# Rebalancing the Fourier and gate stages of a fused GFNet and gMLP block: one DMA queue in written order, copies moved between VectorE and ScalarE, the last Fourier step moved into the main loop

## The chip, the cores and the metric

The kernel runs on one core of a Trainium2 chip. The metric is the device time in microseconds, the median of several runs. A profiled execution gives the span from the first to the last instruction, which is a little shorter than the device time. The engines of the core work side by side, each through its own list of instructions in order: TensorE (PE in the profile; PEld is its weight load), VectorE (DVE), ScalarE (ACT), GpSimd (POOL) and SyncE (SP). In this kernel SP does nothing but start transfers. The kernel is written with a tile scheduler: it takes the program, works out which instruction must wait for which, and may reorder the instructions of each engine.

## The reference, cut to what matters

`x` is 2048 x 576, bf16. One branch filters the normalised `x` in the frequency domain, the other is a gated MLP whose gate mixes the 2048 rows. Their product is added to `x`.

```python
def _A_ref(x, w_r, w_i):                      # spectral filter
    X = rfft2(x) * (w_r + 1j * w_i)           # over rows (2048) and columns (576)
    return irfft2(X, s=(2048, 576))

def _B_ref(x, w_in, w_sp, b_sp, w_out):       # Fh = 2304
    z = gelu(x @ w_in)
    z1, z2 = z[..., :Fh], layernorm(z[..., Fh:])
    g = w_sp @ z2 + b_sp[:, None]             # w_sp is 2048 x 2048
    return (z1 * g) @ w_out

xn = layernorm(x)
return x + _A_ref(xn) * silu(_B_ref(xn))
```

## The kernel before

Everything works on 16 row tiles `m` of 128 rows. The stages, by the names in the code:

- `ln1`, `p0`: normalise `x`, transpose it into `xnT`, multiply by the column DFT (`CDSD`), store to `Ad` in HBM.
- `p1`, `p23`, `p4`, `p5`: the 2048-point DFT over rows in two factors, the product with `w_r`, `w_i`, and the way back. Between the steps the data goes through HBM (`Ad`, `Bd`, `Ed`, `Yd`), which reshuffles it.
- `z2`: the gate half, `gelu(xn @ w_in)` and its layernorm, kept in `Z2`.
- `z1`, `main`: for each of 4 blocks `q` of 512 rows and 18 column tiles `fi`: the value half, then `w_sp @ z2`, bias, product into `U`. `outm`: the last matmul, silu, product with the filtered `x`, sum, store.

The parts that the change touches:

```python
sizes = dict(A0=12288, ..., AIN=4*8*L, TT=8*L, BES=2*8*L, ZT=5*512)   # one SBUF arena AR
SLAB = [reg("AIN", 0, 8192)..., reg("A0", 0, 8192)...]                # w_sp, transposed, two blocks
TMP  = [reg("ZT", (3 + i) * 512, 512) for i in range(2)]
...
XC = [load_x(0)]                              # four loads of one row tile, SP queue
nc.sync.dma_start(out=CDSD, ...)
for c in range(1, 4): XC.append(load_x(c))    # four row tiles in one load each
for g in range(2):                            # gate weights, ACT queue
    nc.scalar.dma_start(out=WIN2[:, 0:KS-1, sl], ...)
    nc.scalar.dma_start(out=WIN2[0:KT, KS-1, sl], ...)
nc.scalar.dma_start(out=G1, ...); nc.scalar.dma_start(out=MM, ...)
nc.scalar.dma_start(out=G4, ...); nc.scalar.dma_start(out=CESO, ...)

def ln1(ms):
    ...                                       # bn_stats, bn_aggr on VectorE
    rs = rstd_of(mv, n, f"l1_{n}")            # (var + eps) ** -0.5 on GpSimd
    ...                                       # nm = -mean * rs, two GpSimd instructions
    for i, m in enumerate(ms):
        nc.scalar.activation(out=xn[:, 0:D], in_=XC[...], func=ACT.Identity, bias=nm, scale=rs)
        for ks in range(KS): nc.tensor.transpose(pt[:, ks, :], xn[:, ks*P:(ks+1)*P], ident[:])
        nc.vector.tensor_copy(out=xnT[:, m, :, :], in_=pt[:])

def p0(m):    # 10 matmuls, ScalarE copy into one of 3 STG buffers, SP store to Ad
def p1(ch):   # SP load from Ad; 8 matmuls; copies half ScalarE, half VectorE; SP store to Bd
def p23(ch):  # SP load from Bd; per 2 slices: 2 matmuls, 2 VectorE products with the
              # spectral weights, 4 matmuls, ScalarE copy; SP stores to Ed
def p4(ch):   # SP load from Ed; 3 x 8 matmuls, each group copied into V by VectorE
def p5(j):    # 6 matmuls, ScalarE copy, VectorE sum and difference, 2 SP stores to Yd
def z2(m):
    for n in range(NZC):                      # 6 pieces of 384 columns
        ...                                   # 5 matmuls into ph
        nc.scalar.activation(out=Z2[m][...], in_=ph[:], func=ACT.Gelu_apprx_tanh)
        nc.vector.bn_stats(out=st[:, n, :], in_=Z2[m][...])
    nc.vector.bn_aggr(...); rs = rstd_of(mv, 1, "l2")
    nc.vector.tensor_scalar(out=Z2[m][:], in0=Z2[m][:], scalar1=mean, scalar2=rs, ...)

for ms in ([0], [1], [2, 3], [4, 5, 6, 7], [8, 9, 10, 11], [12, 13, 14, 15]):
    ln1(ms)
    for m in ms: p0(m)
load_w(0); load_w(1)
for ch in range(4): p1(ch)
for ch in range(4): p23(ch)
for ch in range(4): p4(ch)
for m in range(MT): z2(m)
for j in range(MT): p5(j)
load_slab(0); ...; load_slab(1)
nc.sync.dma_start(out=WOUT, ...)
z1(0)
for k in range(NK):                           # NK = 72
    if k + 1 < NK: z1(k + 1)                  # 5 matmuls of 512 columns
    main(k)                                   # 16 matmuls of 512 columns, 2 VectorE instructions
    if fi == 0 and q > 0:
        for i in range(4): outm(q - 1, i)     # 36 matmuls of 288 columns each
        ...
```

The scheduler mixes `z2` into `p1`, `p23` and `p4`, so TensorE has work while a Fourier step waits for its transfer.

Of the kernel before, what the change touches and what calls it, by code (L numbers as in the profile page):

```python
# [80 lines left out]
def kernel(  # L81
# [56 lines left out]
    make_identity(nc, ident[:])  # L138
    mhalf = pers.tile([P, MT], F32)
# [3 lines left out]
                 AIN=4 * 8 * L, TT=8 * L, BES=2 * 8 * L, ZT=5 * 512)  # L143
# [14 lines left out]
    SLAB = [reg("AIN", 0, 8192).rearrange("p (m t) -> p m t", m=MT),  # L158
# [12 lines left out]
    TMP = [reg("ZT", (3 + i) * 512, 512) for i in range(2)]  # L171
# [10 lines left out]
    def load_x(c):  # L182
        t = AIN[c][:, 0:4 * D].rearrange("p (m d) -> p m d", m=4)
        if c == 0:
            for i in range(4):
                nc.sync.dma_start(out=t[:, i, :], in_=xv[:, i, :])
        else:
            nc.sync.dma_start(out=t, in_=xv[:, 4 * c:4 * c + 4, :])
        return t

    XC = [load_x(0)]
# [4 lines left out]
    wv = B_w_in[0:(KS - 1) * P, :].rearrange("(k p) f -> p k f", p=P)  # L196
    for g in range(2):
        sl = slice(g * Fh // 2, (g + 1) * Fh // 2)
        gl = slice(Fh + g * Fh // 2, Fh + (g + 1) * Fh // 2)
        nc.scalar.dma_start(out=WIN2[:, 0:KS - 1, sl], in_=wv[:, :, gl])  # L200
        nc.scalar.dma_start(out=WIN2[0:KT, KS - 1, sl], in_=B_w_in[(KS - 1) * P:D, gl])
    nc.scalar.dma_start(out=G1, in_=cd_g1.ap().rearrange("p (s k) -> p s k", s=N2))
    nc.scalar.dma_start(out=MM, in_=cd_mm.ap().rearrange("p (a k) -> p a k", a=3))
    nc.scalar.dma_start(out=G4, in_=cd_g4.ap().rearrange("p (s k) -> p s k", s=N2))
    nc.scalar.dma_start(out=CESO, in_=cd_ceso.ap().rearrange("p (a c l) -> p a c l", a=NLC, c=2))
# [8 lines left out]
    def ln1(ms):  # L214
        n = len(ms)
        mv = small.tile([P, n, 2], F32, tag=f"mv{n}", bufs=3)
        for i, m in enumerate(ms):
            st = small.tile([P, 2, 6], F32, tag="st1", bufs=4)
            for h in range(2):
                nc.vector.bn_stats(out=st[:, h, :], in_=XC[m // 4][:, m % 4, h * H2:(h + 1) * H2])  # L220
            nc.vector.bn_aggr(out=mv[:, i, :], in_=st[:])
        rs = rstd_of(mv, n, f"l1_{n}")
        nm = small.tile([P, n], F32, tag=f"nm{n}", bufs=3)
        nc.gpsimd.tensor_tensor(out=nm[:], in0=mv[:, :, 0], in1=rs[:], op=ALU.mult)
        nc.gpsimd.tensor_scalar(out=nm[:], in0=nm[:], scalar1=-1.0, scalar2=0.0, op0=ALU.mult, op1=ALU.add)
        for i, m in enumerate(ms):
            xn = XN[m % 3]
            nc.scalar.activation(out=xn[:, 0:D], in_=XC[m // 4][:, m % 4, :], func=ACT.Identity,  # L228
                                 bias=nm[:, i:i + 1], scale=rs[:, i:i + 1])
            pt = psh.tile([P, KS, P], BF16, tag="h")  # L230
            for ks in range(KS):
                nc.tensor.transpose(pt[:, ks, :], xn[:, ks * P:(ks + 1) * P], ident[:])  # L232
            nc.vector.tensor_copy(out=xnT[:, m, :, :], in_=pt[:])  # L233
# [15 lines left out]

    def p1(ch):  # L250
        ain = AIN[ch]
        nc.sync.dma_start(out=ain, in_=rowv(Ad)[:, ch * 8 * L:(ch + 1) * 8 * L])
        av = ain.rearrange("p (s l) -> p s l", s=8)
        bs = BES[ch % 2]
        bv = bs.rearrange("p (s l) -> p s l", s=8)
        for i in range(0, 8, 2):
            pa = psa.tile([P, 2, 512], F32, tag="a")
            for j in range(2):
                nc.tensor.matmul(pa[:, j, 0:L], lhsT=G1[:, ch * 8 + i + j, :], rhs=av[:, i + j, :], start=True, stop=True)
            if i % 4 == 0:  # L260
                nc.scalar.activation(out=bv[:, i:i + 2, :], in_=pa[:, :, 0:L], func=ACT.Identity)
            else:
                nc.vector.tensor_copy(out=bv[:, i:i + 2, :], in_=pa[:, :, 0:L])
        nc.sync.dma_start(out=rowv(Bd)[:, ch * 8 * L:(ch + 1) * 8 * L], in_=bs)
# [7 lines left out]

    def p23(ch):
        ain = AIN[ch].rearrange("p (h l) -> p h l", h=8)
        nc.sync.dma_start(out=ain, in_=colv(Bd)[:, ch * 8:(ch + 1) * 8, :])
        for i in range(0, 8, 2):
            hh = ch * 8 + i
            if hh % 4 == 0 and hh >= 8:
                load_w(hh // 4)
            wt = WCH[(hh // 4) % 2]  # L280
            tt = TT[(i // 2) % 2]
            pa = psa.tile([P, 2, 512], F32, tag="a")
            for j in range(2):
                nc.tensor.matmul(pa[:, j, 0:L], lhsT=MM[:, 0, :], rhs=ain[:, i + j, :], start=True, stop=True)
            for c in range(2):
                nc.vector.tensor_tensor(out=tt[:, c, :, :], in0=pa[:, :, 0:L], in1=wt[:, c, hh % 4:hh % 4 + 2, :], op=ALU.mult)  # L286
            pb = psa.tile([P, 2, 512], F32, tag="a")
            for j in range(2):
                for c in range(2):
                    nc.tensor.matmul(pb[:, j, 0:L], lhsT=MM[:, 1 + c, :], rhs=tt[:, c, j, :], start=(c == 0), stop=(c == 1))  # L290
            es = BES[ch % 2].rearrange("p (h l) -> p h l", h=8)
            nc.scalar.activation(out=es[:, i:i + 2, :], in_=pb[:, :, 0:L], func=ACT.Identity)
            if i % 4 == 2:
                nc.sync.dma_start(out=colv(Ed)[:, hh - 2:hh + 2, :], in_=es[:, i - 2:i + 2, :])

    def p4(ch):
        ain = AIN[ch]
        nc.sync.dma_start(out=ain, in_=rowv(Ed)[:, ch * 8 * L:(ch + 1) * 8 * L])
        av = ain.rearrange("p (s l) -> p s l", s=8)
        for lc in range(NLC):  # L300
            pa = psa.tile([P, 2, 4, P], F32, tag="a")
            for i in range(8):
                nc.tensor.matmul(pa[:, i // 4, i % 4, :], lhsT=av[:, i, LC0[lc]:LC0[lc] + P], rhs=G4[:, ch * 8 + i, :],
                                 start=True, stop=True)
            nc.vector.tensor_copy(out=V[:, lc, :, ch * 8:ch * 8 + 8, :].rearrange("p c s t -> p s c t"),  # L305
                                  in_=pa[:].rearrange("p a s (c t) -> p (a s) c t", c=2))
# [16 lines left out]

    def z2(m):
        st = small.tile([P, NZC, 6], F32, tag="st2")
        mv = small.tile([P, 1, 2], F32, tag="mvz")
        for n in range(NZC):
# [4 lines left out]
            nc.scalar.activation(out=Z2[m][:, n * ZC:(n + 1) * ZC], in_=ph[:], func=ACT.Gelu_apprx_tanh)  # L332
            nc.vector.bn_stats(out=st[:, n, :], in_=Z2[m][:, n * ZC:(n + 1) * ZC])  # L333
        nc.vector.bn_aggr(out=mv[:, 0, :], in_=st[:])
# [4 lines left out]
    for ms in ([0], [1], [2, 3], [4, 5, 6, 7], [8, 9, 10, 11], [12, 13, 14, 15]):  # L339
        ln1(ms)  # L340
        for m in ms:
            p0(m)
    load_w(0)
    load_w(1)
    for ch in range(4):
        p1(ch)
    for ch in range(4):
        p23(ch)
    for ch in range(4):
        p4(ch)  # L350
    for m in range(MT):
        z2(m)
    for j in range(MT):
        p5(j)

    wspv = B_w_sp.rearrange("t (b p) -> t b p", p=P)

    def load_slab(q):
        for i in range(4):
            t0 = q * 512 + i * P  # L360
            nc.sync.dma_start_transpose(out=SLAB[q % 2][:, :, i * P:(i + 1) * P], in_=wspv[t0:t0 + P, :, :])

    load_slab(0)
    nc.sync.dma_start(out=BB, in_=B_b_sp.rearrange("(a s) -> a s", a=1).to_broadcast((P, S)))
    for i in range(2):
        nc.gpsimd.memset(WIN1[i][KT:P, KS - 1, :], 0.0)
    load_slab(1)
    nc.sync.dma_start(out=WOUT, in_=B_w_out.rearrange("(f p) d -> p f d", p=P))

    steps = [(q, fi) for q in range(NQ) for fi in range(FT)]  # L370

    def z1(k):
# [3 lines left out]
        if fi % WG == 0:  # L376
            fs = slice(fi * P, (fi + WG) * P)
            nc.sync.dma_start(out=wb[:, 0:KS - 1, :], in_=wv[:, :, fs])
            nc.sync.dma_start(out=wb[0:KT, KS - 1, :], in_=B_w_in[(KS - 1) * P:D, fs])
# [34 lines left out]
    z1(0)  # L414
    NK = len(steps)
    for k in range(NK):
        q, fi = steps[k]
        if k + 1 < NK:
            z1(k + 1)
        main(k)  # L420
        if fi == 0 and q > 0:
            if q + 1 < NQ:
                pass
            for i in range(4):
                outm(q - 1, i)
            if q + 1 < NQ:
                load_slab(q + 1)
    for i in range(4):
        outm(NQ - 1, i)
# [30 lines left out]
```

## Time and profile before

| | before |
|---|---|
| device time, median of 6 runs | 598.63 us (598.07 to 601.3) |
| span of the profiled execution | 596.9 us |
| TensorE busy | 546.5 us, 92% |
| VectorE busy | 243.7 us, 41% |
| ScalarE busy | 145.8 us, 24% |
| GpSimd busy | 23.8 us, 4% |
| moved by the transfers | 59.46 MB |

A share of busy time is an average over the stages. The page also has a view of the span in 40 slices, in which VectorE stands at 9 tenths for several slices of the first third, and at 2 or 3 tenths in the last two thirds. A matmul's duration in the profile is its latency; neighbours overlap, so rates are taken from runs of many matmuls in the chain of work. A wait is given with the engine and line that waited, what it waited for, the sum in us, how often, and the longest.

### The profile page before, as it was taken

To read this page: it belongs to the slowest core of one execution; us is meant where nothing else is said; L and a number is where in the kernel's file an instruction comes from. 1 tells how busy PE (TensorE), PEld (TensorE's weight loads), DVE (VectorE), ACT (ScalarE), POOL (GpSimd) and SP (SyncE) were. 2 spreads that over 40 slices of the span, in tenths; PEclk is the share of its full clock that TensorE was granted. 3 is DMA by queue.
4 is the path that set the end of the run, shared out by engine and by line. 5 is a ranking of instruction groups with operands and counts; after the bars stand their busy time and mean duration, and the time that the engine had idled before them with its cause. 6 is when DMAs were issued, how large, how long until landed. Compare 5 with 4: busy or idle time off the path is not lost.

```text
span 596.9 us, 7781 instructions
## 1 busy us (share of the span) xinstructions
PE 546.5 (92%) x3128; PEld 299.5 (50%) x3128; DVE 243.7 (41%) x468; ACT 145.8 (24%) x258; POOL 23.8 (4%) x69
## 2 busy tenths in 40 slices
PE   0299899997979959999999999999999999999996
PEld 0177455555645424444744444674444475444465
DVE  3522789997976202222322222232222223222223
ACT  0386556662533101111111111111111101111101
POOL 4200100010010000000000000000000000000000
PEclk9999999998989969999999999999999999999999
DMA  9923686654715871113731111751111114111002
GB/s 312 329 82 95 235 239 170 162 160 163 140 30 116 199 226 31 30 31 78 155 87 30 40 50 31 129 136 56 31 30 31 30 33 118 30 31 30 1 9 71
DMA packets 80964, 59.46 MB, mean 100 GB/s; under 512 B 36768, under 2 KB 75552, under 8 KB 80672
## 3 DMA queue, kind: packets, MB, share of 16 engines
q1 hardware_dynamic: 79136, 53.68, 33.6%
q10 hardware_dynamic: 1792, 5.29, 2.6%
q8 instruction: 24, 0.39, 0.3%
q14 instruction: 12, 0.10, 0.1%
HBM read 38.74 MB, written 11.82 MB: 85 GB/s over the span
## 4 chain that ended last, share of the span: by engine, by line
PE 78%; DMA 8%; DVE 8%; ACT 2%; issue 1%; POOL 1%; SPq 1%; ACTq 0%; DVEq 0%; POOLq 0%
PE pg L390 41%; PE ph L382 13%; PE po L404 12%; PE ph L330 5%; PE pa L241 3%; DVE st L333 3%; DMA AR<-in_A_x_dram 2%; DVE AR L305 2%; DMA AR<-in_B_w_out_dram 2%; DVE AR L286 1%; PE pa L314 1%; PE pb L290 1%; DMA Ed<-AR 1%; DVE z L336 1%; DMA AR<-in_A_w_i_dram 1%
## 5 line engine op out<-in xcount | busy, mean ns | idle before, releaser
L390 PE MATMUL pg<-AR,z 128*128 128x512 bf16 x1152 | 262.8, 380 | 0.0
L390 PEld LDWEIGHTS <-z 128*128 128x128 bf16 x1152 | 113.1, 98 | 135.3 <-issue 1.9
L393 DVE TENSOR_TENSOR AR<-pg,AR 128x512 bf16<-128x512 f32 x72 | 49.8, 691 | 236.9 <-PE pg L390 236.9
L384 ACT ACTIVATE AR<-ph 128x512 bf16<-128x512 f32 x72 | 43.0, 597 | 272.2 <-PE ph L382 272.2
L382 PE MATMUL ph<-xnT,AR 128*128 128x512 bf16 x360 | 91.2, 384 | 0.0
L330 PE MATMUL ph<-RW,xnT 128*128 128x384 bf16 x480 | 88.2, 328 | 0.0
L404 PE MATMUL po<-AR,RW 128*128 128x288 bf16 x576 | 72.4, 288 | 6.7 <-DMA AR<-in_B_w_out_dram 6.7
L404 PEld LDWEIGHTS <-RW 128*128 128x128 bf16 x576 | 56.7, 98 | 22.5 <-issue 7.0
L330 PEld LDWEIGHTS <-xnT 128*128 128x128 bf16 x480 | 46.8, 98 | 26.4 <-issue 0.9
L332 ACT ACTIVATE z<-ph 128x384 bf16<-128x384 f32 x96 | 46.9, 491 | 41.7 <-PE ph L330 41.5
L382 PEld LDWEIGHTS <-AR 128*128 128x128 bf16 x360 | 35.6, 99 | 41.9 <-issue 0.8
L333 DVE BATCH_NORM_STATS2 st<-z 128x6 f32<-128x384 bf16 x96 | 48.1, 542 | 8.2 <-ACT z L332 7.9
L394 DVE TENSOR_TENSOR RW<-AR 128x512 bf16<-128x512 bf16 x72 | 30.6, 425 | 7.4 <-DVE AR L393 0.5
L409 DVE SCALAR_TENSOR_TENSOR AR<-TH,po 128x576 bf16<-128x576 f32 x16 | 12.1, 755 | 46.4 <-ACT TH L408 46.4
L232 PE MATMUL pt<-ident,AR 128*128 128x128 bf16 x80 | 6.3, 230 | 26.4 <-ACT AR L228 26.3
L408 ACT ACTIVATE TH<-po 128x576 f32<-128x576 f32 x16 | 10.4, 651 | 76.5 <-PE po L404 76.5
L241 PE MATMUL pa<-AR,xnT 128*128 128x289 bf16 x160 | 22.6, 298 | 0.3 <-ACT AR L244 0.2
L286 DVE TENSOR_TENSOR AR<-pa,AR 128x578 bf16<-128x578 f32 x32 | 22.6, 746 | 0.1
L232 PEld LDWEIGHTS <-AR 128*128 128x128 bf16 x80 | 5.1, 102 | 27.5 <-ACT AR L228 27.3
L241 PEld LDWEIGHTS <-xnT 128*128 128x128 bf16 x160 | 15.7, 101 | 5.8 <-DVE xnT L233 0.6
L314 PE MATMUL pa<-AR 128*128 128x289 bf16 x96 | 14.9, 298 | 3.8 <-DVE AR L320 3.5
L220 DVE BATCH_NORM_STATS2 st<-AR 128x6 f32<-128x288 bf16 x32 | 12.6, 428 | 12.8 <-DMA AR<-in_A_x_dram 12.8
(40 smaller groups left out, 212.0 us busy)
## 6 DMA issues: line engine op xcount, KB each, us to landing
AR<-in_B_w_in_dram SPq DMA_DIRECT2D x24, 384.0 KB, 3.5
AR<-in_A_x_dram SPq DMA_DIRECT2D x20, 144.0 KB, 2.7
AR<-in_B_w_out_dram SPq DMA_DIRECT2D x1, 2592.0 KB, 10.5
AR<-in_A_w_r_dram SPq DMA_DIRECT2D x16, 144.5 KB, 3.5
AR<-in_A_w_i_dram SPq DMA_DIRECT2D x16, 144.5 KB, 3.9
Ad<-AR SPq DMA_DIRECT2D x16, 144.5 KB, 2.7
AR<-Ad SPq DMA_DIRECT2D x4, 578.0 KB, 5.6
Bd<-AR SPq DMA_DIRECT2D x4, 578.0 KB, 2.8
```

What stands on the lines that cost most here:

```text
L241: nc.tensor.matmul(pa[:, c, 0:L], lhsT=xnT[:, m, ks, :], rhs=CDSD[:, ks, c, :], start=(ks == 0), stop=(ks == KS - 1))
L286: nc.vector.tensor_tensor(out=tt[:, c, :, :], in0=pa[:, :, 0:L], in1=wt[:, c, hh % 4:hh % 4 + 2, :], op=ALU.mult)
L314: nc.tensor.matmul(pa[:, c, 0:L], lhsT=V[:, lc, c, 2 * j:2 * j + 2, :], rhs=CESO[:, lc, c, :], start=(lc == 0), stop=(lc == NLC - 1))
L330: nc.tensor.matmul(ph[:], lhsT=xnT[:, m, ks, :], rhs=WIN2[:, ks, n * ZC:(n + 1) * ZC], start=(ks == 0), stop=(ks == KS - 1))
L332: nc.scalar.activation(out=Z2[m][:, n * ZC:(n + 1) * ZC], in_=ph[:], func=ACT.Gelu_apprx_tanh)
L333: nc.vector.bn_stats(out=st[:, n, :], in_=Z2[m][:, n * ZC:(n + 1) * ZC])
L382: nc.tensor.matmul(ph[:].rearrange("p (a t) -> p a t", a=4), lhsT=wb[:, ks, (fi % WG) * P:(fi % WG + 1) * P], rhs=xnT[:, 4 * q:4 * q + 4, ...
L384: nc.scalar.activation(out=Z1T[k % 3], in_=ph[:], func=ACT.Gelu_apprx_tanh)
L390: nc.tensor.matmul(pg[:], lhsT=Z2[m][:, fi * P:(fi + 1) * P], rhs=SLAB[q % 2][:, m, :], start=(m == 0), stop=(m == MT - 1))
L393: nc.vector.tensor_tensor(out=tmp, in0=pg[:], in1=BB[:, q * 512:(q + 1) * 512], op=ALU.add)
L394: nc.vector.tensor_tensor(out=U[k % NU], in0=tmp, in1=Z1T[k % 3], op=ALU.mult)
L404: nc.tensor.matmul(po[:, h, 0:H2], lhsT=U[(q * FT + fi) % NU][:, i * P:(i + 1) * P], rhs=WOUT[:, fi, h * H2:(h + 1) * H2], start=(fi == 0) ...
```

## The change

It is a set of edits around one idea: spread the work of the stages before the main loop over the engines anew, and fix the order of the transfers by hand.

1. All loads go through the SP queue. ScalarE no longer starts any. SP keeps the order in which the program is written (`manual_schedule`): `x` first, then the gate weights, `G1`; `MM`, `G4`, `CESO` and the spectral weights come later.
2. In `ln1` the reciprocal root is a ScalarE Sqrt and a VectorE reciprocal. The normalising moves from ScalarE to VectorE, the copy of the transposed tile from VectorE to ScalarE. GpSimd has no part in it.
3. All copies of `p1` go to ScalarE; every second copy of `p4` goes to ScalarE.
4. `p5` moves behind `z2` into the first eight steps of the main loop, two per step. `WOUT` and the second `w_sp` block are loaded after that, from step 8 on.
5. The first `w_sp` block, the bias and the first value weights are loaded during `p4`. For that the arena is laid out anew: `SLAB[0]` leaves the first two `AIN` buffers free, a `PAD` is added, `p4` uses two `AIN` buffers instead of four, and one `TMP` buffer moves.
6. Loads are split from the work that uses them, and value weights are loaded two groups ahead.

There is also a version of `z2` that takes its sums on ScalarE; it is switched off (`on_act = False`).

```diff
-                 AIN=4 * 8 * L, TT=8 * L, BES=2 * 8 * L, ZT=5 * 512)
+                 AIN=4 * 8 * L, PAD=3568, TT=8 * L, BES=2 * 8 * L, ZT=4 * 512)
-    SLAB = [reg("AIN", 0, 8192)...
+    SLAB = [reg("AIN", 2 * 8 * L, 8192)...
-    TMP = [reg("ZT", (3 + i) * 512, 512) for i in range(2)]
+    TMP = [reg("ZT", 3 * 512, 512), reg("BES", 2 * KS * WG * P, 512)]
...
-        if c == 0:
+        if c < 2:
             for i in range(4):
-                nc.sync.dma_start(out=t[:, i, :], in_=xv[:, i, :])
+                nc.sync.dma_start(out=t[:, i, :], in_=xv[:, 4 * c + i, :])
...
-        nc.scalar.dma_start(out=WIN2[:, 0:KS - 1, sl], in_=wv[:, :, gl])
-        nc.scalar.dma_start(out=WIN2[0:KT, KS - 1, sl], in_=B_w_in[(KS - 1) * P:D, gl])
-    nc.scalar.dma_start(out=G1, ...)      # and MM, G4, CESO
+        nc.sync.dma_start(out=WIN2[:, 0:KS - 1, sl], in_=wv[:, :, gl])
+        nc.sync.dma_start(out=WIN2[0:KT, KS - 1, sl], in_=B_w_in[(KS - 1) * P:D, gl])
+    nc.sync.dma_start(out=G1, ...)
...
-        rs = rstd_of(mv, n, f"l1_{n}")
-        nm = ...                          # two GpSimd instructions
+        nc.scalar.activation(out=rs[:], in_=mv[:, :, 1], func=ACT.Sqrt, bias=eps[:], scale=1.0)
+        nc.vector.reciprocal(out=rs[:], in_=rs[:])
-            nc.scalar.activation(out=xn[:, 0:D], in_=XC[m // 4][:, m % 4, :], func=ACT.Identity, ...)
+            nc.vector.tensor_scalar(out=xn[:, 0:D], in0=XC[m // 4][:, m % 4, :], scalar1=mv[:, i, 0:1],
+                                    scalar2=rs[:, i:i + 1], op0=ALU.subtract, op1=ALU.mult)
-            nc.vector.tensor_copy(out=xnT[:, m, :, :], in_=pt[:])
+            nc.scalar.activation(out=xnT[:, m, :, :], in_=pt[:], func=ACT.Identity)
...
 def p1:
-            if i % 4 == 0: ScalarE copy, else: VectorE copy
+            nc.scalar.activation(out=bv[:, i:i + 2, :], in_=pa[:, :, 0:L], func=ACT.Identity)
 def p4:
-            nc.vector.tensor_copy(out=V[...], in_=pa[...])
+            if (ch * NLC + lc) % 2 == 0: VectorE copy
+            else: nc.scalar.activation(out=vd, in_=vs, func=ACT.Identity)
...
+    with tc.manual_schedule(engines={mybir.EngineType.SP}):
+        for ms in ([0], [1], [2, 3], [4, 5], [6, 7], [8, 9, 10, 11], [12, 13, 14, 15]):
+            ln1(ms)
+            for m in ms: p0(m)
+        MM; p1_read(0..3); G4; CESO       # loads
+        for ch in range(4):
+            if ch < 2: load_w(ch)
+            p1(ch)
+        p23_read(0..3)
+        for ch in range(4): p23(ch)       # each load_w now right after the half that frees its buffer
+        p4_read(0); p4_read(1); load_win1(0); slab_part(0, 0)
+        for ch in range(4):
+            p4(ch)
+            if ch < 2: p4_read(ch + 2); slab_part(0, ch + 1)
+        slab_part(0, 3); BB; load_win1(1)
+        for m in range(MT): z2(m)
+        z1(0)
+        for k in range(NK):
+            q, fi = steps[k]
+            if q == 0 and 2 * fi < MT:
+                p5(2 * fi); p5(2 * fi + 1)
+            if q == 0 and 2 * fi == MT:
+                WOUT; load_slab(1)        # loads
+            if k + 1 < NK: z1(k + 1)
+            main(k)
+            if fi % WG == 1 and k // WG + 2 < NK // WG: load_win1(k // WG + 2)
+            if fi == 0 and q > 0:
+                for i in range(4): outm(q - 1, i)
+                if q + 1 < NQ: load_slab(q + 1)
+        for i in range(4): outm(NQ - 1, i)
```

## The prediction, made before the changed kernel ran

> **What bounds the kernel now.** I read the waits of TensorE first, because it is busy for 92% of the span. A row gives who waited, for what, the sum in us, the times, the longest wait.
>
> ```profile
> PE pt L232 <- ACT AR L228: 26.3, 1, 26.3
> PE po L404 <- DMA AR<-in_B_w_out_dram: 6.7, 1, 6.7
> PE pa L314 <- DVE AR L320: 3.5, 1, 3.5
> PE pa L303 <- DMA AR<-Ed: 3.3, 1, 3.3
> PE pa L259 <- DMA AR<-Ad: 2.0, 1, 2.0
> ```
>
> The largest is the head: TensorE waits 26.3 us for the first normalised tile (L228, ScalarE). The timeline of ScalarE's queue at the start shows why.
>
> ```profile
> 0.72 0.47 ACTq L200 DMA_DIRECT2D RW<-in_B_w_in_dram  x1
> ...
> 8.94 0.62 ACTq L202 DMA_DIRECT2D AR<-c_g  x1
> 17.06 0.34 ACTq L203 DMA_DIRECT2D AR<-c_mm  x1
> 22.78 0.33 ACTq L204 DMA_DIRECT2D AR<-c_g  x1
> 23.65 0.33 ACTq L205 DMA_DIRECT2D AR<-c_ceso  x1
> 24.06 1.28 ACT L228 ACT_TABLE_LOAD   x1 [24.06 <-DMA AR<-in_A_w_i_dram]
> ```
>
> ScalarE takes its list in order, eight load starts stand ahead of its first activation, and the later starts wait for earlier transfers. So it is free only at 24.06 us, although the first tile's statistics began at 3.21.
>
> Then the busy time in five stretches cut from the chain of work: `p1` with `z2`; `p23` with `z2`; the wait for `Ed`; `p4` and the rest of `z2`; and `p5` with the first main steps. Columns: TensorE, weight loads, VectorE, ScalarE, GpSimd.
>
> ```profile
> 54.40:82.30 27.90, 25.45 (x157) 15.12 (x156) 20.60 (x37) 18.14 (x34) 2.24 (x6) 1.00 0.55 196
> 82.30:128.10 45.80, 43.62 (x281) 25.99 (x280) 43.46 (x78) 27.16 (x53) 4.86 (x13) 1.00 0.68 176
> 128.10:138.75 10.65, 7.35 (x47) 4.21 (x44) 8.42 (x18) 4.98 (x10) 1.90 (x5) 1.00 0.66 207
> 138.75:173.60 34.85, 31.33 (x244) 20.74 (x244) 30.86 (x49) 14.19 (x29) 3.16 (x9) 0.95 0.42 102
> 173.60:220.00 46.40, 39.44 (x201) 20.36 (x202) 18.32 (x41) 8.77 (x19) 0.55 (x1) 0.87 0.71 183
> ```
>
> In `p23` and `p4` VectorE is as full as TensorE, and ScalarE is at 59% and 41%. The chain runs through VectorE there, with one piece of 11.40 us of `p4` copies (L305). After 220 us TensorE works without a gap, so that nothing but its own work counts. The chain around 216 us shows the last loss:
>
> ```profile
> 217.93 2.13 PE ph L382 x5
> 220.06 4.09 PE pg L390 x16
> 224.15 1.08 PE ph L382 x5
> 225.23 3.45 PE pg L390 x16
> ```
>
> After its wait for `WOUT` TensorE needs 2.13 us for what then takes 1.08.
>
> **What the Trainium skill says.** *DMA: Bandwidth & Descriptors*, "Issuing engines are not separate DMA queues": transfers started by ScalarE and SP run on the same 16 engines, and a second issuer saves only issue time. The trace agrees: between 4 and 25 us both queues together moved 353 GB/s with the engines full, and the second `x` tile was counted only at 7.87 us because gate weights ran beside it. *ScalarE: Activation LUTs*, "What ACT_TABLE_LOAD costs": about 1283 ns per load, and 0.833 ns per element for an activation. The trace has 1.283 us, and (652 - 413) / (578 - 289) = 0.83 ns. There are two table loads before and two after, since all Sqrt come ahead of the first Gelu in the built order. *VectorE: DVE Perf Modes*, "The perf-mode tier table": a bf16 `tensor_scalar` in SBUF has a faster tier than `tensor_tensor`. Here 2304 elements took 878 ns in L336 and 576 took 458 ns in a `tensor_tensor` (L411). *TensorE: Matmul & The Clock Gate*, "The HAM clock gate": after idling the array runs at half clock for some 3.4 us, which fits 2.13 against 1.08.
>
> **Rates.** TensorE, from long runs in the chain: 163 ns per `z2` matmul (38 in 6.19), 126 per `p0` matmul (20 in 2.52), 88 in `p4` (16 in 1.41), about 130 in `p1`, `p23`, `p5`, 56 per transpose. A main step is 3.45 + 1.08 = 4.53 us, an `outm` block 17.64. All TensorE work is 78.0 (`z2`) + 20.2 (`p0`) + 4.5 (transposes) + 4.2 + 12.5 + 8.4 + 12.5 (`p1`, `p23`, `p4`, `p5`) + 326.4 (72 steps) + 70.6 (4 `outm`) = 537 us. The change leaves this alone; it can gain only from the 596.9 - 537 = 60 us around it.
>
> **The head and `p0`.** SP now brings four `x` tiles, `CDSD`, then the rest of `x`. At some 350 GB/s `x` and `CDSD` (3.1 MB) are there at 13 us, gate weights and `G1` at about 24. VectorE begins at 3.2, does statistics of four tiles (0.8 us each) before its first normalising, so the first transposes come near 7 and `p0` near 9. Then three engines carry similar loads. VectorE per tile: 0.8 + about 0.27 (a quarter of 878 plus a fixed part; estimate) = 1.07, or 17 us. ScalarE up to its first Gelu in the built order: 16 transposed tiles at 0.70 (from 174 + 0.83 x 640 ns), 5 `p0` copies at 0.65, 7 short Sqrt at 0.2 = 16 us. TensorE follows ScalarE to about 26 us. Then 11 tiles of `p0` (110 x 126 ns = 13.9) and 14 `z2` matmuls (2.3) remain. That ends at 42 us; before it was 54.4. Gain 12.4, not 20, because transposes now wait for ScalarE.
>
> **`p1`.** From the end of `p0` to the first `p1` matmul took 62.6 - 54.4 = 8.2 us (copy, store, load). It stays, so 50. The built order has 151 `z2` and 32 `p1` matmuls up to `p23`: 24.6 + 4.2 = 29 us, with about 1 of waiting: 80, where before it was 83.8 with only 91 `z2` matmuls done. That is 60 x 163 ns = 9.8 us of `z2` taken out of the crowded later stages. ScalarE has 16 x 0.65 + 30 x 0.49 = 25 us here, which fits in 29.
>
> **`p23`.** 96 and 173 matmuls (96 and 176 before): 40.7 us of TensorE. VectorE has 32 x 0.71 = 22.7 and 5.8 tiles of `z2` at about 4.2 (6 x 0.463 + 0.23 + 0.88 + part of a GpSimd wait) = 24, so 47. Nothing was moved here; VectorE keeps the bound and it lasts 44 us as before: 124.
>
> **`p4`.** Before, 10.65 us passed until `Ed` was back; the last store had two other loads ahead of it. Now nothing is ahead: 10, of which 40 `z2` matmuls hide 6.5. So 134. Then 96 x 88 ns + 39 x 163 ns = 14.8, with VectorE only at 6 x 1.15 and ScalarE at 6 x 1.02 us of copies. For the third and fourth load, which wait for a freed buffer behind a `w_sp` transpose (2.3 us to issue, 5.1 to land), I add 2.5. The last 22 `z2` matmuls take 3.6. End of `z2`: 155. Before: 173.6.
>
> **Main loop.** 12.5 + 326.4 + 70.6 = 409.5; before it took 591.7 - 173.6 = 418.1. The 8.6 above the work are the `WOUT` wait, the slow clock after it and the `p5` waits. `WOUT` now starts ten steps (45 us) before its use and lands in 10.5, so they go. I leave 1.5 for the first `p5` and the last normalising: 566. The tail took 5.2; SP in written order starts the last loads of `outm` only after the preceding store, so 6.2. Span 572.2, device time 1.7 more: 574. By stages the gain is 18.6 + 7.1 - 1.0 = 24.7 us.
>
> **Rivals.** (a) One queue becomes the bottleneck. `Ad` stores queue behind gate weights until 24 us, `Bd` stores behind 1.2 MB of spectral weights and `G4`, `CESO`; written order lets nothing pass. For it: each start may have to wait for an earlier transfer, as ScalarE's starts did. Against it: `p0` makes most of its stores after 24 us, and 59 `z2` matmuls stand in the built order where `Bd` is stored. It would cost 5 to 12: 580 to 586. (b) ScalarE or VectorE becomes the head's bound more than I think, with TensorE in fragments at half clock. For it: 50 transposes stand in a row, each group behind a ScalarE copy. Cost 4 to 8: about 580. (c) VectorE is relieved further, since it enters `p23` without the `p1` copies: `p23` at 41 and `p4` without load waits would give 565. (d) New waits in the main loop, as `WOUT`, four transposes and a weight load stand in one queue at step 8. The weight load is due six steps (27 us) later, the rest needs some 21; a miss costs 2 to 5.
>
> **Range and chances.** The head and the `WOUT` wait are single waits with a visible cause; they make more than half of the gain. The middle is uncertain by some 8 us either way. Range 564 to 586. 2% faster is 586.7, which only (a) with (b) would miss: 0.90 faster, 0.08 same, 0.02 slower.
>
> **What would show it.** Right: the first transposes near 7 us, the end of `p0` near 42, first `p23` matmul near 80, `z2` over near 155, then no wait of TensorE above 2 us and no `WOUT` wait. Wrong: a TensorE wait for `Ad`, `Bd` or `Ed` over 5 us, SP waits in front of stores in the first 80 us, or main steps above 4.53 us.

## The result, and the profile after

| | before | changed |
|---|---|---|
| device time, median | 598.8 us (597.2 to 601.3) | 570.73 us (569.63 to 572.52) |
| ratio | | 0.9529, 95% interval 0.9512 to 0.9546 |
| span of the profiled execution | 596.9 us | 567.9 us |

The time lies 3.3 us under the predicted 574, well inside the range of 564 to 586. The waits of TensorE after the change, in the same columns as before:

```profile
PE pt L230 <- DVE AR L226: 11.6, 4, 6.7
PE pa L304 <- DMA AR<-Ed: 2.4, 2, 2.0
PE pa L259 <- DMA AR<-Ad: 2.2, 1, 2.2
PE pb L287 <- DVE AR L283: 1.5, 3, 0.5
```

The wait for `WOUT` and the waits in `p5` are gone. The head is down from 26.3 to 6.7 us, but 4.9 us of other waits for normalised tiles have come up behind it: the sum in the first row is 11.6 in 4 waits.

The stages of the changed kernel, columns as before (TensorE, weight loads, VectorE, ScalarE, GpSimd; then TensorE's granted clock). The rows are: the second half of `p0`; the wait for `Ad`; `p1`; `p23`; the wait for `Ed`; `p4` and the rest of `z2`; everything from the end of `z2` to TensorE's last matmul.

```profile
24.80:45.00 20.20, 19.44 (x147) 14.24 (x148) 2.04 (x5) 12.35 (x20) 0.00 (x0) 0.92 0.30 85
45.00:53.20 8.20, 6.00 (x37) 3.42 (x36) 5.19 (x10) 4.27 (x9) 0.75 (x2) 1.00 0.60 168
53.20:83.60 30.40, 29.53 (x184) 17.89 (x185) 20.44 (x40) 22.53 (x46) 3.71 (x10) 1.00 0.68 241
83.60:127.10 43.50, 41.98 (x273) 25.40 (x274) 41.78 (x76) 26.04 (x50) 4.11 (x11) 1.00 0.61 165
127.10:135.60 8.50, 6.51 (x41) 3.72 (x38) 7.08 (x15) 4.36 (x9) 1.89 (x5) 1.00 0.48 155
135.60:153.60 18.00, 16.30 (x158) 11.27 (x159) 14.72 (x22) 11.05 (x18) 1.48 (x4) 1.00 1.07 243
153.60:562.60 409.00, 408.96 (x2185) 213.34 (x2182) 119.97 (x225) 59.88 (x104) 0.74 (x2) 1.00 0.28 70
```

In `p23` VectorE is still as full as TensorE (41.78 against 41.98 us). In `p4` it is not any more: 14.72 against 16.30, before 30.86 against 31.33. The last row is TensorE without a gap, 409.0 us; the prediction's sum of its work there was 409.5.

Set side by side, in us from the start of the span (each time is that of TensorE's matmuls of the named line):

| | before | predicted | changed |
|---|---|---|---|
| first transpose | 26.3 | 7 | 6.7 |
| `p0` over | 54.4 | 42 | 44.8 |
| first `p1` | 62.6 | 50 | 53.2 |
| first `p23` | 83.8 | 80 | 83.6 |
| `p23` over | 128.1 | 124 | 127.1 |
| first `p4` | 138.7 | 134 | 135.6 |
| `z2` over | 166.7 (taken as 173.6) | 155 | 153.6 |
| last matmul | 591.7 | 566 | 562.6 |
| end of span | 596.9 | 572.2 | 567.9 |

The row of `z2` is the one where the prediction had its zero wrong. The two lines that show it for the kernel before are TensorE's matmuls of `z2` and VectorE's normalising of the gate tiles, with the shortest, median and longest duration in ns, then the first and last start in us:

```profile
L330 PE MATMUL ph<-RW,xnT x480: 323/326/524, 54.2 to 166.5; 128*128 128x384 bf16 x160
L336 DVE TENSOR_SCALAR z<-z,mv,rs x16: 867/879/880, 61.7 to 174.2; 128x2304 bf16<-128x2304 bf16 x16
```

and the same two for the changed kernel:

```profile
L341 PE MATMUL ph<-RW,xnT x480: 324/326/528, 26.4 to 153.3; 128*128 128x384 bf16 x160
L362 DVE TENSOR_SCALAR z<-z,mv,rs x16: 871/879/880, 49.9 to 156.0; 128x2304 bf16<-128x2304 bf16 x16
```

Before, TensorE was through with `z2` at 166.7 us and VectorE came after it 7.5 us later, with a backlog. After the change the two are 2.4 us apart. So the stages up to `z2` gave 166.7 - 153.6 = 13.1 us, and everything from there to the last matmul 425.0 - 409.0 = 16.0 us.

The table also shows where the head's gain of 9.6 us went: at the end of `p23` only 1.0 is left of it. It is not lost. Between the first `p1` and the first `p23` matmul stand 151 `z2` matmuls now and 91 before, and behind the first `p4` matmul 61 are left where 128 were. The time came back there, as 18.0 us against 28.0.

### The profile page after: what moved, and what is told of

It reads as the page before. It is cut to its first block, busy times and chain, and to the rows that moved or that the text cites. A ratio compares the mean times of both kernels' runs of the same rounds, so it can differ in the third digit from the quotient of the medians.

```text
span 567.9 us, 7760 instructions
## 1 busy us (share of the span) xinstructions
PE 541.3 (95%) x3128; PEld 298.9 (53%) x3128; DVE 231.1 (41%) x462; ACT 153.3 (27%) x279; POOL 15.7 (3%) x45
## 4 chain that ended last, share of the span: by engine, by line
PE 85%; DVE 6%; DMA 5%; ACT 2%; issue 1%; POOL 0%; SPq 0%; DVEq 0%; ACTq 0%
PE pg L391 44%; PE ph L383 14%; PE po L405 12%; PE ph L341 7%; PE pa L239 3%; PE pa L319 2%; DVE AR L283 2%; DVE st L348 1%; DMA AR<-in_A_x_dram 1%; PE pb L287 1%; DVE AR L309 1%; PE pa L259 1%; DVE st L219 1%; DMA AR<-Ed 1%; DMA AR<-Bd 1%
## 5 line engine op out<-in xcount | busy, mean ns | idle before, releaser
L383 PE MATMUL ph<-xnT,AR 128*128 128x512 bf16 x360 | 89.5, 379 | 0.0
L405 PE MATMUL po<-AR,RW 128*128 128x288 bf16 x576 | 71.2, 286 | 0.0
L348 DVE BATCH_NORM_STATS2 st<-z 128x6 f32<-128x384 bf16 x96 | 48.8, 546 | 27.8 <-ACT z L347 27.8
L383 PEld LDWEIGHTS <-AR 128*128 128x128 bf16 x360 | 35.1, 98 | 40.7 <-DMA AR<-in_B_w_in_dram 0.5
L230 PE MATMUL pt<-ident,AR 128*128 128x128 bf16 x80 | 6.7, 243 | 11.6 <-DVE AR L226 11.6
L362 DVE TENSOR_SCALAR z<-z,mv,rs 128x2304 bf16<-128x2304 bf16 x16 | 14.0, 878 | 8.7 <-POOL rs L210 8.7
L287 PE MATMUL pb<-AR 128*128 128x289 bf16 x64 | 13.3, 289 | 1.5 <-DVE AR L283 1.5
L322 ACT ACTIVATE TH<-pa 128x289 f32<-128x289 f32 x16 | 6.6, 413 | 28.3 <-PE pa L319 28.2
## 6 DMA issues: line engine op xcount, KB each, us to landing
AR<-in_B_w_out_dram SPq DMA_DIRECT2D x1, 2592.0 KB, 12.6
```

Of the source, the lines that this page charges most:

```text
L348: nc.vector.bn_stats(out=st[:, n, :], in_=zc)
L383: nc.tensor.matmul(ph[:].rearrange("p (a t) -> p a t", a=4), lhsT=wb[:, ks, (fi % WG) * P:(fi % WG + 1) * P], rhs=xnT[:, 4 * q:4 * q + 4, ...
L405: nc.tensor.matmul(po[:, h, 0:H2], lhsT=U[(q * FT + fi) % NU][:, i * P:(i + 1) * P], rhs=WOUT[:, fi, h * H2:(h + 1) * H2], start=(fi == 0) ...
```

## The experiments

All ratios are to the kernel before, run beside it on the same chip. Theory T, as the prediction had it: the head is held by ScalarE's own load starts; VectorE's copies and the wait for `WOUT` are the rest. Rivals: the new `ln1` (R1), the order by hand (R2), copies that are absorbed (R3).

| run | us | ratio, 95% interval |
|---|---|---|
| changed kernel | 570.73 | 0.9529 (0.9512 to 0.9546) |
| before, loads by SP | 591.06 | 0.9872 (0.9824 to 0.9920) |
| before, `WOUT` at step 8 | 588.02 | 0.9846 (0.9833 to 0.9860) |
| before, `p5` in the main loop and `WOUT` at step 8 | 585.35 | 0.9772 (0.9726 to 0.9819) |
| before, loads by SP and `p5` in the main loop | 576.85 | 0.9660 (0.9631 to 0.9688) |
| changed, old `ln1` | 570.86 | 0.9526 (0.9487 to 0.9565) |
| changed, old copies | 572.39 | 0.9583 (0.9564 to 0.9602) |
| changed, `p5` in one block | 573.09 | 0.9593 (0.9574 to 0.9613) |
| changed, SP ordered by the scheduler | 575.57 | 0.9606 (0.9567 to 0.9645) |
| changed, `WOUT` two steps before its use | 569.48 | 0.9530 (0.9507 to 0.9553) |
| changed, `ln1` in pairs | 570.89 | 0.9564 (0.9543 to 0.9584) |
| changed, pairs and root on GpSimd | 569.25 | 0.9543 (0.9522 to 0.9563) |
| changed, once more | 568.67 | 0.9529 (0.9507 to 0.9550) |

**Loads by SP, alone.**

```diff
-    nc.scalar.dma_start(out=WIN2[...] ...   # six lines: WIN2 (2, in a loop), G1, MM, G4, CESO
+    nc.sync.dma_start(out=WIN2[...] ...
```

> The kernel before with one edit: the loads that ScalarE started are started by SP. Theory T (the long head comes from ScalarE standing behind its own load starts): TensorE's first wait falls from 26.3 to under 10 us, p0 is over at 40 to 44 us, time about 586 to 588. Rival R1 (the head is shortened by the new ln1, not by the loads): the first wait stays above 20 us and the time above 593.

The head fell as T says. The waits of TensorE in this run:

```profile
PE pt L232 <- ACT AR L228: 12.0, 6, 10.5
PE po L404 <- DMA AR<-in_B_w_out_dram: 8.4, 1, 8.4
PE pa L314 <- DVE AR L320: 4.0, 3, 3.4
```

But the 15.8 us of the head were only 4.7 at the end of `p0` (49.7) and 9.4 in the span (587.5), and 591 us is 3 more than expected. `z2` was over on TensorE at 155.8 us, nearly as early as in the changed kernel; yet the last gate tile was normalised from 163.5 on, 7.7 us later. An earlier TensorE ran into the same VectorE backlog (it waited 4.0 us in `p5`) and the same `WOUT` wait (8.4 us). R1's numbers are excluded: with `ln1` as it was, the first wait is 10.5.

**The old `ln1` in the changed kernel.**

```diff
-        nc.scalar.activation(out=rs[:], in_=mv[:, :, 1], func=ACT.Sqrt, ...); nc.vector.reciprocal(...)
+        rs = rstd_of(mv, n, f"l1_{n}"); nm = -mean * rs          # GpSimd, as before
-            nc.vector.tensor_scalar(out=xn ...) ; nc.scalar.activation(out=xnT ...)
+            nc.scalar.activation(out=xn ...)    ; nc.vector.tensor_copy(out=xnT ...)
```

> The changed kernel with ln1 as before (root on GpSimd, normalising on ScalarE, copy of the transposed tile on VectorE). T: the new ln1 is worth little, since ScalarE's load stays at 0.86 + 0.65 us per tile against 0.65 + 0.65 now: 570 to 574. R1: the head grows by 6 us or more, 577 or above.

No difference: 0.9526 against 0.9529. TensorE's first transpose came at 15.9 us instead of 6.7, and `p0` was over at the same time, 44.6. What starts 9 us sooner is given back before `p0` ends: with the old form TensorE was busy for 27.8 of the 28.75 us from its first transpose on, with the new one for 32.0 of 38.3, and 4.9 of the idle time were further waits for normalised tiles. The new form also did 14 `z2` matmuls on the way, nine of them at half clock. R1 falls.

**SP left to the scheduler.**

```diff
-    with tc.manual_schedule(engines={mybir.EngineType.SP}):
+    if True:
```

> The changed kernel with SP left to the scheduler, as all other engines are. T (the order by hand is a means, not the source of the gain): 568 to 574. Rival R2 (the written order makes the gain): 578 or more, with TensorE waits for Bd or Ed of several us.

Between the two: 0.9606, which is 0.8% or 4.6 us slower than the changed kernel. The scheduler put two `w_sp` transposes in front of the last store to `Ed`. SP's queue in this run (start, duration):

```profile
113.56 0.58 SPq L293 DMA_DIRECT2D Ed<-AR  x1
115.16 5.06 SPq L369 DMA_TRANSPOSE AR<-in_B_w_sp_dram  x2
120.32 0.53 SPq L293 DMA_DIRECT2D Ed<-AR  x1
120.90 2.88 SPq L369 DMA_TRANSPOSE AR<-in_B_w_sp_dram  x1
125.20 0.81 SPq L296 DMA_DIRECT2D AR<-Ed  x2
```

By the chain of work, the last store landed 4.82 us after SP began to start it. The first `p4` matmul came 11.2 us after `p23` here, against 8.5 in the changed kernel. TensorE's waits for `Ad`, `Bd` and `Ed` sum to 8.4 us against 5.4. The order by hand is worth something, but it is not the source of the gain. The run doesn't test SP's queue alone, though: with the one line TensorE's list came out differently too. `p23` was over at 118.2 us instead of 127.1, and 127 `z2` matmuls instead of 61 were left behind the first `p4` one. How the 4.6 us divide between the two is open.

**`p5` and `WOUT` into the main loop, alone.**

```diff
-    for j in range(MT): p5(j)
-    load_slab(1); nc.sync.dma_start(out=WOUT, ...)
     for k in range(NK):
+        if q == 0 and 2 * fi < MT: p5(2 * fi); p5(2 * fi + 1)
+        if q == 0 and 2 * fi == MT: nc.sync.dma_start(out=WOUT, ...); load_slab(1)
```

> The kernel before with one part of the change: p5 two per step in the first eight steps of the main loop, WOUT and the second w_sp block loaded from step 8. T: the wait for WOUT (6.7 us), the slow clock after it (about 3) and the wait in p5 (3.5) go, everything before 173 us is as it was: 588 to 591. Rival: the p5 pairs bring waits of their own into the main steps and half of it is lost: 593 to 596.

More than expected: 585.35, a gain of 13.7 us where the prediction had 7.1 for this part. That is the second place where its wrong zero shows. Which half of the edit does it, and why, the next two runs tell.

**`WOUT` at step 8, `p5` left where it was.**

```diff
-    load_slab(1); nc.sync.dma_start(out=WOUT, ...)
     for k in range(NK):
+        if q == 0 and 2 * fi == MT: nc.sync.dma_start(out=WOUT, ...); load_slab(1)
```

> The kernel before with one edit: WOUT and the second w_sp block are loaded from step 8 of the main loop; p5 stays in one block ahead of it. Theory T4 (the wait for WOUT was not a late load but nine matmuls of outm that the scheduler had put some 14 steps ahead of the rest, in front of TensorE's list while the load was on its way; now they stand at step 18): the wait of 6.7 us and the slow clock after it go, 588 to 590, so that of the 13.5 us of the p5 run only 3 to 5 belong to p5 itself. Rival: p5 is the larger part, 593 to 596.

T4 holds: 588.02, so 9.2 us of the 13.7, and 4.5 are left for `p5` (by the two intervals, between about 1 and 8). The chain of work of the kernel before shows what the wait was:

```profile
205.05 10.52 DMA AR<-in_B_w_out_dram
215.61 2.32 PE po L404 x9
...
283.07 16.54 PE po L404 x135
```

`outm` needs all 18 column tiles of a block and could not be finished before 283 us. But the scheduler had put 9 of the block's 144 matmuls at 215 us, where TensorE's list in order stood still until the load was there. With the load later in the program, the 9 matmuls stay with the other 135: here the first one came at 271.1 us, and no wait for `WOUT` is left. By itself this run leaves a rival, since the scheduler let the load start at 194.9 us, 10 us sooner than before. The run with `p5` in the main loop closes it: there the load started at 217.3, later than in the kernel before (205.05), the first `outm` matmul came at 270.6, and nothing waited. The load did not have to be early; it had to keep those matmuls from being put ahead of it.

**`WOUT` late.**

```diff
-            if q == 0 and 2 * fi == MT: nc.sync.dma_start(out=WOUT, ...); load_slab(1)
+            if q == 0 and 2 * fi == MT: load_slab(1)
+            if k == FT: nc.sync.dma_start(out=WOUT, ...)
```

> The changed kernel with WOUT loaded right before its first use, at step 18. T: TensorE waits the whole 10 to 11 us of the landing and then runs some us at half clock: 582 to 586. Rival: the transfer hides behind what stands between: 571 to 574.

T as I had put it fails: 0.9530, no loss at all. SP reached the load ahead of TensorE:

```profile
242.10 0.54 SPq L465 DMA_DIRECT2D AR<-in_B_w_out_dram  x1
253.60 17.80 PE L405 MATMUL po<-AR,RW 128*128 128x288 bf16 x144
```

It started 11.5 us before the first `outm` matmul and took 11.0 to land. So this run did not make the load late enough to show a full wait. It does show that the lead of the changed kernel, where the load started at 202.6 us and 50 us before its first use, is not needed.

**`p5` in one block in the changed kernel.**

```diff
-            if q == 0 and 2 * fi < MT: p5(2 * fi); p5(2 * fi + 1)
+        for j in range(MT): p5(j)          # ahead of z1(0)
```

> The changed kernel with p5 in one block between z2 and the main loop, as before; WOUT and the second w_sp block stay at step 8. T3 (16 p5 steps in a row run at the pace of ScalarE copy, VectorE sum and difference and the two PSUM buffers): 574 to 577. Rival R4 (p5 lost time before only because VectorE came late with the gate tiles, which is mended by the other parts): 570 to 572.

573.09, which is 0.67% or 3.8 us slower than the changed kernel, between the ranges of R4 (up to 572) and T3 (from 574). The two intervals do not meet, so the loss is real and R4 falls. T3 had the pace wrong, though. SP's queue in this run between 150 and 180 us (start, duration, number of starts):

```profile
157.56 20.83 SPq L327 DMA_DIRECT2D Yd<-AR  x31
```

and, from the waits of the same stretch, VectorE's wait for a result buffer (sum, times, longest):

```profile
DVE AR L324 <- DMA Yd<-AR: 4.4, 9, 0.8
```

Each `p5` step has two stores, and SP needs 0.594 us in the median to start one. 31 starts take 20.8 us without a gap, and the three result buffers come free at that pace; from 157.6 to 170.2 us the chain of work runs mostly through these starts and the landing of two stores. So SP as the pace is read from the trace; no run changed the starts alone. Spread over eight main steps the same 32 stores left no wait of TensorE in `p5`.

**The old copies in the changed kernel.**

```diff
 p1: half of the copies back on VectorE;   p4: all copies back on VectorE
```

> The changed kernel with the copies as before: p1 half on VectorE, p4 all on VectorE. Theory T2 (VectorE's backlog, 12 more copies or about 6.0 + 6.9 us, reaches TensorE when the last gate tiles and V are late for p5 and the first main step): 575 to 579, with TensorE waits for VectorE between 130 and 165 us. Rival R3 (the backlog is absorbed, since only ScalarE frees the gate matmuls' PSUM): 570 to 572.

Neither: 572.39, 0.57% or 3.2 us slower than the changed kernel. The direction is T2's. VectorE's last gate tile moved from 156.0 to 161.8 us, but TensorE waited only 1.6 us in `p5` and 0.7 for the tile. Its `z2` was over at 152.8, even a little sooner than in the changed kernel (153.6), so the loss lies behind it. Most of the backlog is absorbed.

**Loads by SP and `p5` in the main loop together.**

> The kernel before with the two edits of the first two single runs together: loads by SP instead of ScalarE, and p5, WOUT and the second w_sp block moved into the main loop. If the parts add (7.7 and 13.5 us): 578, which leaves some 7 us for the moved copies and the order by hand. T2: it stays at 577 to 580, TensorE waiting for VectorE's last gate tiles at the first main step. R3: more than the sum, since the head's gain is no longer lost behind p5: 572 to 575.

576.85, a gain of 20.3 us by the ratio; the single gains add to 7.7 + 13.7 = 21.4. Its chain from 136 to 168 us has no piece of TensorE; it is VectorE's, with short pieces of GpSimd for the roots:

```profile
136.13 11.40 DVE AR L305 x10
147.53 0.93 DVE st L333 x2
...
166.93 0.89 DVE z L336
...
167.87 0.39 PE pg L385
```

So TensorE's first main step ends with the last gate tile, as T2 says. But TensorE's own wait for that tile was 1.7 us, and the time does not tell T2 from plain addition: 576.85 lies just under T2's range, and its interval takes in the 577.4 of the sum. The step from here to the changed kernel, 0.9660 to 0.9529, is 1.4% or 7.8 us; old copies and SP order, each undone by itself, cost 3.2 and 4.6.

**Two attempts to go further**, with the changed kernel beside them (568.67).

```diff
-        for ms in ([0], [1], [2, 3], [4, 5], [6, 7], [8, 9, 10, 11], [12, 13, 14, 15]):
+        for ms in ([0], [1], [2, 3], [4, 5], [6, 7], [8, 9], [10, 11], [12, 13], [14, 15]):
# second run: also the root by rstd_of on GpSimd instead of Sqrt and reciprocal
```

Both have six instead of three buffers for the small statistics tiles.

> The changed kernel with the last two ln1 groups of four split into pairs. If TensorE's waits for VectorE's normalising (11.6 us in sum, 4.9 of it after the first) come from groups that must be complete before the root: p0 ends 2 us sooner, 568 to 569.5. Rival: ScalarE's copies and the tile arrival set the pace: 570 to 571.

> The changed kernel with pairs in ln1 and the root on GpSimd as before the change; normalising stays on VectorE and the copy on ScalarE. The Sqrt no longer stands in ScalarE's list behind copies, and one table load goes: p0 ends near 41 us instead of 45, 566.5 to 568.5. Rival: 110 matmuls of p0 still stand behind all transposes and the end of p0 does not move: 570 to 571.

> The changed kernel once more, unedited, as the yardstick for the runs of this call: 570 to 571.5.

Neither is faster. Pairs alone took 2.2 us more than the unedited kernel beside them and end `p0` at 45.7 us, no sooner. With the root on GpSimd `p0` is over at 41.4 us as expected, and the first `p4` matmul comes at 132.7 against 133.6. But the stretch from there to the end of `z2` takes 20.4 us instead of 18.4, since the scheduler has left more `z2` matmuls for it (74 instead of 61). An early end of `p0` is worth nothing if the work that could fill the later waits is not moved up with it. The unedited kernel itself ended `p0` at 44.8 us in one profile and at 43.4 in another, so differences of 1.5 us there say little. No version here beats the changed kernel.

## Why the prediction was right, point by point

**What bounds the kernel: right.** TensorE's work was put at 537 us and left alone; the changed span has 537 + 31. The 409.5 us of work for the main loop were 409.0. That the end came out so near is in part luck: the stages missed in both directions. The kernel was 3.6 us late against the forecast at the first `p23` matmul and 1.4 early at the end of `z2`; the main loop and the tail were 2.0 and 0.9 shorter than forecast.

**The head: right in cause, too good in size.** The first transpose came at 6.7 (7 predicted), and the run with loads by SP alone shows the cause. "That ends at 42 us" was 44.8, a gain of 9.6 instead of 12.4. The chain of work of the changed kernel shows the rest:

```profile
20.10 3.69 ACT xnT L231 x6
...
24.28 0.44 DVE AR L226
24.76 1.82 PE pt L230 x20
26.58 2.72 PE ph L341 x9
29.30 2.51 PE pa L239 x20
31.81 0.81 PE ph L341 x5
32.62 10.04 PE pa L239 x80
42.70 0.66 ACT AR L242
43.41 1.43 PE pa L239 x10
```

The transposes were through at 26.6 us (26 predicted), behind ScalarE's copies as forecast: 0.62 us each in a row against 0.70. The other 11 tiles of `p0` and 14 `z2` matmuls then needed 18.3 us where 16.2 were due. Nine of these `z2` matmuls took 2.72 us, at half clock, where 1.46 were due, and TensorE stood 0.8 us for one ScalarE copy at 42.7. So of rival (b), "TensorE in fragments at half clock", 1.3 us came true, and 0.8 as a wait. That the old `ln1` ends `p0` just as soon was not foreseen.

**`p1` and `p23`: right.** 8.4 us to the first `p1` (8.2), 30.4 for `p1` (30), 43.5 for `p23` (44). The 151 `z2` matmuls of `p1` were counted rightly. VectorE kept its bound in `p23`; of rival (c) only the second half came, `p4` almost without load waits.

**`p4`: right in kind, too careful.** 8.5 us until `Ed` was back (10); 18.0 to the end of `z2` (20.9). The 2.5 us added for the third and fourth load were not there: TensorE's second wait for `Ed` was 0.4. That these stages gain through VectorE was half right: the backlog was there, but most of it is absorbed, and the copies are worth 3.2 us.

**The zero of `z2` and the main loop: wrong, and the two errors cancelled.** "End of `z2`: 155. Before: 173.6" took VectorE's last gate tile for the end of TensorE's `z2`. TensorE had been through at 166.7. So the gain up to there was 13.1 and not 18.6, and the "8.6 above the work" of the main loop were 425.0 - 409.5 = 15.5: about 5.9 in the stretch with `p5`, 9.6 around `WOUT` and the slow clock. The predicted absolute times, 155 and 566, were built from the work and not from the difference, so they held (153.6, 562.6).

**`WOUT`: right that the wait goes, wrong why.** "`WOUT` now starts ten steps (45 us) before its use" was not the reason. The load in the kernel before landed some 67 us ahead of the bulk of `outm`; nine matmuls had been placed at 215 us, and waited. The two `WOUT` runs show both halves. The slow clock after the wait lasted some 5.7 us (an estimate from the chain: 2.32 + 2.13, and twice 4.09 - 3.45), longer than the 3.4 that the prediction names. Half of it, some 2.9 us, was lost; with the wait of 6.7 that makes the 9.6.

**`p5`: its cost before was put down to VectorE's waits (3.5 us).** That wait was there, and ended with VectorE's backlog at 173.6 us. Behind it came a cost that the prediction did not have, SP's starts of the stores, 24 of the 32 without a gap in the kernel before:

```profile
173.58 16.85 SPq L322 DMA_DIRECT2D Yd<-AR  x24
```

By the runs the place of `p5` is worth 3.8 us in the changed kernel and about 4.5 in the one before. How that divides between the backlog and the starts is not shown.

**The tail:** 5.3 us, not 6.2; the last loads were there in time.

**Rival (a), one queue as the bottleneck,** did not come: waits for `Ad`, `Bd` and `Ed` sum to 5.4 us, none above 2.2. **Rival (d)** did not come: no wait of TensorE in the main loop.

Summed by single runs: loads 7.7, place of the `WOUT` matmuls 9.2, `p5` 4.5, copies 3.2, SP order 4.6: 29.2 us, against 28.1 measured. They were not all taken from the same base, and the interval of each is 1 to 3 us to either side, so the agreement is rough and proves little. Edits 5 and 6, the early loads for the main loop, were undone in no run of their own. A trace of what they do is there: in the kernel before with `p5` in the main loop, TensorE waited 2.1 us for value weights (1.7 with loads by SP as well), and in the changed kernel it does not.

What stays open is why old and new `ln1` end `p0` at the same time, 44.6 and 44.8 us, in different ways; it may be chance. One part is visible. In the changed kernel the Sqrt for the last four tiles stood behind the six copies shown above and ran at 23.6 us. With pairs and the root on GpSimd `p0` ended at 41.4 us, with pairs alone at 45.7, in one profile each.

## What to carry to other kernels

Fix a stage's end by one engine's own instructions, first and last start, and not by where the chain of work changes its line: an engine with a backlog can finish a stage long after the one whose time counts. When an engine waits for a transfer, look in its list for whether the waiting instruction belongs there at all; a scheduler may have put a few of a group ahead of a load that the group does not need for a long time. An engine freed early is worth only what can follow it: here 15.8 us at the head came to 7.7 until the backlog and the waits further down were also gone.

## What the runs showed of the hardware that was not expected

SP's own time to start a transfer counts. The median for one start in the changed kernel was 0.360 us for the stores to `Ad` and 0.564 for those to `Yd`; for a `w_sp` transpose it was 2.57 (2.27 in the kernel before). With `p5` in one block, 31 starts kept SP busy for 20.8 us without a gap, although a store landed in 2.1 us in the median.

Loading `WOUT` (2592 KB) took 10.5 us to land in the kernel before, 12.6 in the changed kernel beside four transposes, and 11.0 where it was loaded late; over all runs it was 10.2 to 13.4.
